# State outputs in four array quarters, the last logits at once, and the surrounding tables

## Chip, cores and metric

The kernel runs on one core of one Trainium2 chip. The metric is the device time of one execution in microseconds; lower is better. The time before is the median of three runs.

## What is computed

The reference is a retention layer (linear attention with a decaying state, written as a loop over time) followed by a mixture of experts in which every token goes to exactly one expert:

```python
# B, H, S, D = 4, 8, 768, 64
for t in range(S):
    state = gamma * state + k[:, :, t] (x) v[:, :, t]
    y[:, :, t] = scale * q[:, :, t] . state
x = y as (B*S, H*D) = (3072, 512)
logits = x @ w_gate                      # 8 experts
order = argsort(-logits.flatten())       # greedy, 384 tokens per expert
for each expert e:
    out[its tokens] = relu(x[its tokens] @ w1[e]) @ w2[e]    # 512 -> 1024 -> 512
```

## The kernel before

**Retention in chunks.** A unit is one batch of the four and one chunk of 128 time steps of the six, so there are 24 units, chunk by chunk (`units`, number 4c + b). Heads go in four pairs: 128 partitions hold the 64 features of two heads. The first eight units are worked one at a time (groups 0 to 7), the other sixteen in pairs (groups 8 to 15). Within a group g, TensorE (PE) does in this order: `scores` of the group that comes next (L297: keys times queries, two row halves of the array side by side), `outputs` of g (L326: queries times the state `T`, which is a 128 x 128 block-diagonal tile for each head pair), `mix` of g (L339: values times masked scores, two column halves, added to the same PSUM tile `yp`), and the state's increment (L353, into `sp`). All are float32, and each such matmul is two instructions in the trace. After every second group the gate of a finished chunk follows (L402, four batches side by side in four column quarters), and one group later its logits are turned (L408).

**The other engines.** VectorE (DVE) multiplies the scores by the decay mask (L300, `am`), adds `sp` to the state (L359, one instruction for each half of the partitions, since only the diagonal blocks of `T` are kept up), and turns some of the finished outputs into rows of `xs` in DRAM (`row_blocks`, L390). GpSimd (POOL) scales queries and keys (L308 `qs`, L304 `ks`). ScalarE (ACT) copies `yp` out of PSUM (L346; in the last chunk half of it goes by DVE, L343 and L344).

**The queue.** All loads and row stores are issued by SyncE (SP), in program order: the loads of the units eight ahead (L268; `ld` has eight buffers) behind a group's work, then four stores for each row block that `ROWS` names for this group (L394). `ROWS = {8: 2, 9: 2, 10: 3, ...}` means two row blocks behind group 8, and so on.

**Logits and search.** `aside` runs between `outputs` and `mix`. It turns the logits of a chunk and prepares the search, and once the first `KNOWN` = 3 chunks are known it finds their largest and smallest logit (`span_parts`: `over_tokens`, `over_partitions`, `grids`), one part at a time, and makes from it the grid of thresholds on which the search counts. If a count never fits, a flag sends the kernel through a slower exact path (`settle`). In the last chunk `gate_last` computes logits unit by unit, straight with tokens on partitions (L367: eight matmuls for two units, 8 columns each), behind the other work of group 15 for units 20 and 21, and after `mix` for 22 and 23. Then the first count is made (L496), and the search for the first expert's threshold runs while PE turns the ten row blocks that are left (`BESIDE`, `rows_out`, L373) and does warming matmuls (`fill`).

**The experts.** From about 124 us on, the eight experts run their two products on PE. The change does not touch this part but for its start, where `HOT` warming matmuls run until the first rows of `xs` are fetched.

Of the kernel before, what the change touches and what calls it, by code (L numbers as in the profile page):

```python
# [7 lines left out]
F32 = mybir.dt.float32  # L8
# [4 lines left out]
AF = mybir.ActivationFunctionType  # L13
# [25 lines left out]
PARTS = 5  # L39
WARM = (10, 4, 4, 4, 0)  # L40
QB = (6, 6, 6)
KNOWN = 3
DEEP = 8
ROWS = {8: 2, 9: 2, 10: 3, 11: 1, 12: 3, 14: 3}
HOT = 22
BESIDE = ((4, 0), (1, 0), (4, 0), (1, 0), (0, 6), (0, 10))
LEFT = sum(k for k, _ in BESIDE)
BETWEEN = 1
BITS = (6, 6, 5, 5, 5, 5)
SHIFT = tuple(32 - sum(BITS[:i + 1]) for i in range(len(BITS)))  # L50
# [3 lines left out]
def tile_retention_moe(ctx: ExitStack, tc: tile.TileContext, qkv, wg, idm, w1, w2,  # L54
# [12 lines left out]
        return cs[:, o:o + w]  # L67

    ident = consts.tile([128, 128], F32, name="ident")
    wgf = consts.tile([128, HP, 32], F32, name="wgf")  # L70
    sw = ctx.enter_context(tc.tile_pool(name="sw", bufs=1))

    onesb = sw.tile([128, 128], BF, name="onesb")
# [164 lines left out]

    yctx = ExitStack()
    yk = yctx.enter_context(tc.tile_pool(name="yk", bufs=1, side="right"))  # L240
    xo = yctx.enter_context(tc.tile_pool(name="xo", bufs=6, side="right"))
    rctx = ExitStack()
    ld = rctx.enter_context(tc.tile_pool(name="ld", bufs=DEEP))
    rc = rctx.enter_context(tc.tile_pool(name="rc", bufs=1))
# [3 lines left out]
    dm = rc.tile([128, 2, HP, C], F32, name="dm")  # L248
    qtb = rc.tile([128, NC, HP, C], F32, name="qtb")
    ktb = rc.tile([128, NC, H], F32, name="ktb")  # L250
    T = [rc.tile([128, HP, 128], F32, name=f"T{b}") for b in range(B)]
    LD, YS = {}, {}
    warm = rc.tile([128, 256], BF, name="warm")
    nc.vector.memset(warm, 0.0)
# [60 lines left out]

    yps = {}

    def outputs(us):

        c = units[us[0]][1]  # L320
        for u in us:
            yp = yps[u] = rp.tile([128, HP, C], F32, name="yp", bufs=2)
            if c:
# [4 lines left out]
            else:  # L328
                busy(WARM[u + 1], yp[:, 0:2, :].rearrange("p a b -> p (a b)"))

    def mix(us):

        c = units[us[0]][1]
        for u in us:
            b, am, yp = units[u][0], st[u][0], yps.pop(u)
            v_ = LD[u][:, 2].rearrange("p (h d) -> p h d", h=H)
            for pr in range(HP):
                for s in range(2):
                    nc.tensor.matmul(yp[64 * s:64 * s + 64, pr, :], v_[:, 2 * pr + s, :], am[:, s, pr, :],  # L339
                                     start=(not c and pr == 0), stop=(pr == HP - 1), skip_group_check=True)  # L340
            YS[b, c] = yk.tile([128, HP, C], F32, name=f"ys{b}_{c}")
            if c == NC - 1:
                nc.scalar.activation(YS[b, c][:, 0:2], yp[:, 0:2], AF.Copy)  # L343
                nc.vector.tensor_copy(YS[b, c][:, 2:4], yp[:, 2:4])  # L344
            else:
                nc.scalar.activation(YS[b, c], yp, AF.Copy)  # L346
        if c < NC - 1:
            sp = rp.tile([128, 2, HP, D], F32, name="sp")
            for i, u in enumerate(us):
                v_ = LD[u][:, 2].rearrange("p (h d) -> p h d", h=H)  # L350
                for pr in range(HP):
                    for s in range(2):
# [8 lines left out]
    lt5 = []  # L361

    def gate_last(b):
        if not b:
            lt5.append(rp.tile([128, 64, E], F32, name="sp"))
        for pr in range(HP):
            nc.tensor.matmul(lt5[0][:, b, :], YS[b, NC - 1][:, pr, :], wgf[:, pr, 0:E], start=(pr == 0),  # L367
                             stop=(pr == HP - 1))
# [10 lines left out]
    def row_out(pr_, i):  # L379
        b, c = units[i]  # L380
        xr = xo.tile([128, DM], F32, name="xr")
        nc.scalar.activation(blocks(xr), pr_.rearrange("p (b a r) -> p b a r", a=4, b=HP), AF.Copy)
        t0 = (b * NC + c) * 128
        nc.sync.dma_start(xs[t0:t0 + 128, :], xr)

    def row_blocks(i):

        b, c = units[i]
        xr = xo.tile([128, DM], F32, name="xr")
        nc.vector.transpose(xr.rearrange("p (t b r) -> p b t r", t=4, b=HP),  # L390
                            YS[b, c].rearrange("p b (t c) -> p b t c", t=4))
        t0 = (b * NC + c) * 128
        for a in range(4):
            nc.sync.dma_start(xs[t0:t0 + 128, 128 * a:128 * a + 128].rearrange("(t c) f -> c t f", t=4),  # L394
                              xr[32 * a:32 * a + 32].rearrange("p (t f) -> p t f", t=4))

    def gate(c):

        gl = rp.tile([128, 512], F32, name="gl")
        for pr in range(HP):  # L400
            for b in range(B):
                nc.tensor.matmul(gl[32 * b:32 * b + 32, 0:C], wgf[:, pr, :], YS[b, c][:, pr, :], start=(pr == 0),  # L402
                                 stop=(pr == HP - 1), skip_group_check=True)
        nc.scalar.activation(gs[c % 2], gl[:, 0:C], AF.Copy)

# [18 lines left out]
    m0, a0, oh0, cmp0 = prep_tiles()  # L424
    parts, whole, ended = None, [], None
    rowed = 0
    nu = len(units)
    groups = [[u] for u in range(2 * B)] + [[u, u + 1] for u in range(2 * B, nu, 2)]

    def aside():  # L430

        nonlocal parts, whole, ended
        if ended is not None:
            c, ended = ended, None
            logit(c)
            if c == 0:
                consts_on_chip()
            cols = slice(c, COLS, NC)
            best(L[:, cols], cols, m0, oh0)()
            codes(cols, oh0, a0)  # L440
            whole.append(cols)
            if c == KNOWN - 1:
                parts = list(span_parts(rc, rp))
        if parts:
            parts.pop(0)()
        elif parts == []:
            for cols in whole:
                reach(cols, B, m0, cmp0, grid[0])
            whole = []

    with tc.manual_schedule(engines={nc.vector.engine, nc.scalar.engine}):
        decays()
        busy(WARM[0], wp[:, 0:256])
        st[0] = scores(0)
        for g, us in enumerate(groups):
            ahead = groups[g + 1] if g + 1 < len(groups) else ()
            if g != B - 1:
                for u in ahead:
# [12 lines left out]
            if g in (B - 1, B):  # L471
                for u in ahead:
                    st[u] = scores(u)
            for u in us:
                if u + DEEP < nu:
                    load(u + DEEP)
            for _ in range(ROWS.get(g, 0)):
                row_blocks(rowed)
# [12 lines left out]
        f()  # L491
        c0 = rp.tile([1 << QB[0], E], F32, name="gl")
        sg0 = sw.tile([1 << QB[0], E], BF, name="sg")
        order = [c for k in range(NC) for c in range(k, COLS, NC)]
        for k, c in enumerate(order):
            nc.tensor.matmul(c0, cmp0[:, c, :], oh0[:, c, :], start=(k == 0), stop=(k == COLS - 1))  # L496
        nc.vector.tensor_copy(L[:, cols], Lc)
        few(c0, sg0)
    rctx.close()
# [664 lines left out]
```

## Time and profile before

| | us |
|---|---|
| median of three runs | 443.43 (442.95 to 445.39) |
| the profiled execution, its own time | 445.22 |
| its span, first to last instruction | 443.4 |
| retention: the last `mix` is issued out at | about 101.4 |
| first search, rows and fetches | about 103 to 124 |
| experts | about 124 to 443 |

The page gives busy time for each engine: PE 427.8 us (96% of the span), DVE 300.8, ACT 142.2, POOL 142.9. PE is nearly always busy, in every stage; whether a PE instruction costs time must therefore be read from what the next one waited for. Times in the views are counted from the span's start. In a timeline row the second number is the length of the merged piece, and the bracket tells how long the engine idled before it and what ended that.

### The profile page before, as it was taken

What the parts mean: (1) busy time and instruction counts of PE and PEld (TensorE: products, weight loads), DVE (VectorE), ACT (ScalarE), POOL (GpSimd) and SP (SyncE); (2) the same over time, 40 slices, a digit from 0 to 9 for tenths busy, and PEclk for the clock granted to TensorE, in tenths of its full rate; (3) what the DMA queues carried; (4) which work ended last, traced back from release to release, by engine and by line L of the source; (5) the groups of instructions that cost most, each with busy time, mean ns of one, the idle gap of its engine ahead of it and who ended that gap; (6) DMA issues with size and microseconds to landing.
All of it is one profiled execution on the core that took longest, in us unless ns stands there. A gap on an engine that the chain in (4) does not pass through costs nothing.

```text
span 443.4 us, 9124 instructions
## 1 busy us (share of the span) xinstructions
PE 427.8 (96%) x3745; PEld 372.2 (84%) x3747; DVE 300.8 (68%) x714; ACT 142.2 (32%) x221; POOL 142.9 (32%) x154
## 2 busy tenths in 40 slices
PE   9998999899989999999899999999999999999994
PEld 7887999898579778977797798789779989989983
DVE  1668689976798759875885888588668926416500
ACT  1111121203245226313431432434244436326301
POOL 2475665110340170034116216134103615402001
PEclk9999999998999999999999999999999999999999
DMA  7999888744673265138126436425703732831001
GB/s 256 410 414 417 328 261 259 215 92 132 237 231 127 97 191 236 27 133 312 54 95 218 186 120 212 169 59 167 296 26 119 229 152 77 302 143 47 1 25 53
DMA packets 23332, 78.99 MB, mean 178 GB/s; under 512 B 3058, under 2 KB 10866, under 8 KB 16884
## 3 DMA queue, kind: packets, MB, share of 16 engines
q0 software_dynamic: 8592, 46.14, 29.8%
q1 hardware_dynamic: 14692, 32.20, 20.7%
q8 instruction: 31, 0.51, 0.5%
q14 instruction: 17, 0.14, 0.1%
HBM read 65.75 MB, written 12.58 MB: 177 GB/s over the span
## 4 chain that ended last, share of the span: by engine, by line
PE 72%; issue 12%; DVE 9%; POOL 2%; DMA 1%; ACT 1%; POOLq 0%; SPq 0%; DVEq 0%
PE ph L869 22%; PE py L890 21%; PE psm L128 6%; PE sc L297 5%; PE yp L339 4%; PE yp L326 3%; PE ph L837 3%; PE sp L353 2%; DVE am L300 2%; POOL out L898 1%; PE gl L314 1%; DVE w2l L128 1%; POOL wraw L785 1%; DMA xg<-xs,idx 1%; PE gl L402 1%
## 5 line engine op out<-in xcount | busy, mean ns | idle before, releaser
L869 PE MATMUL ph<-xh,w1h 128*128 128x384 f32 x256 | 84.3, 343 | 0.5 <-ACT xh L842 0.5
L869 PE MATMUL ph<-xlo,w1h 128*128 128x384 f32 x256 | 82.7, 337 | 1.7 <-DVE xlo L128 1.5
L869 PE MATMUL ph<-xh,w1l 128*128 128x384 f32 x256 | 82.1, 335 | 0.0
L890 PE MATMUL py<-w2h,hh 128*128 128x512 f32 x192 | 78.9, 411 | 0.0
L890 PE MATMUL py<-w2l,hh 128*128 128x512 f32 x192 | 75.4, 393 | 0.6 <-DVE w2l L128 0.6
L890 PE MATMUL py<-w2h,hl 128*128 128x512 f32 x192 | 75.3, 392 | 0.0
L898 POOL DMA_INDIRECT out<-yo,oix x24 | 28.4, 1182 | 125.4 <-ACT yo L896 124.8
L873 ACT ACTIVATE hh<-ph 128x384 fp32r<-128x384 f32 x64 | 31.4, 491 | 77.5 <-PE ph L869 75.8
L785 POOL DMA_INDIRECT wraw<-w,wix x31 | 34.4, 1109 | 51.1 <-DVE un L128 38.1
L869 PEld LDWEIGHTS ph<-xlo,w1h 128*128 128x128 f32 x256 | 47.5, 188 | 2.3 <-DVE xlo L128 2.3
L869 PEld LDWEIGHTS ph<-xh,w1h 128*128 128x128 f32 x256 | 47.8, 188 | 1.6 <-ACT xh L842 0.7
L869 PEld LDWEIGHTS ph<-xh,w1l 128*128 128x128 f32 x256 | 47.7, 188 | 0.0
L128 DVE SCALAR_TENSOR_TENSOR hl<-ph,hh 128x384 fp32r<-128x384 f32 x64 | 34.7, 552 | 16.9 <-ACT hh L873 16.6
L128 DVE TENSOR_TENSOR w1l<-wraw,w1h 128x1024 fp32r<-128x1024 f32 (+1 forms) x36 | 39.2, 1099 | 7.1 <-ACT w1h L803 7.1
L890 PEld LDWEIGHTS py<-w2h,hl 128*128 128x128 f32 x192 | 36.0, 188 | 7.8
L890 PEld LDWEIGHTS py<-w2l,hh 128*128 128x128 f32 x192 | 36.2, 188 | 7.6 <-DVE w2l L128 1.7
L896 ACT ACTIVATE yo<-py 128x512 f32<-128x512 f32 x24 | 14.4, 598 | 86.6 <-PE py L890 47.1
L890 PEld LDWEIGHTS py<-w2h,hh 128*128 128x128 f32 x192 | 36.1, 188 | 6.9 <-issue 0.7
L824 POOL DMA_INDIRECT xg<-xs,idx x24 | 27.6, 1149 | 43.3 <-PE ph L869 28.7
L128 DVE TENSOR_TENSOR w2l<-wraw,w2h 128x1024 fp32r<-128x1024 f32 x32 | 38.7, 1217 | 1.7 <-ACT w2h L803 1.7
L803 ACT ACTIVATE w1h<-wraw 128x1024 fp32r<-128x1024 f32 (+1 forms) x36 | 33.7, 959 | 7.8 <-DMA wraw<-w,wix 7.8
L300 DVE TENSOR_TENSOR am<-sc,dm 128x512 f32<-128x512 f32 x48 | 30.1, 684 | 5.1 <-PE sc L297 4.7
(145 smaller groups left out, 613.2 us busy)
## 6 DMA issues: line engine op xcount, KB each, us to landing
ld<-qkv SPq DMA_DIRECT2D x19, 1024.0 KB, 9.5
xs<-xr SPq DMA_DIRECT2D x56, 64.0 KB, 3.9
ld<-qkv SPq DMA_DIRECT2D x4, 768.0 KB, 5.8
xs<-xr SPq DMA_DIRECT2D x10, 256.0 KB, 2.8
qtb<-qtab SPq DMA_DIRECT2D x5, 256.0 KB, 11.5
ld<-qkv SPq DMA_DIRECT2D x2, 512.0 KB, 5.2
wraw<-w,wix POOLq DMA_INDIRECT x33
xg<-xs,idx POOLq DMA_INDIRECT x24
```

The source lines that it names most:

```text
L128: return f(o, *a, **k)
L297: nc.tensor.matmul(sc[s][:, pr, :], k_[r, w], q_[r, w], start=True, stop=True)
L300: nc.vector.tensor_tensor(am[:, s], sc[s], dm[:, s], op=OP.mult)
L339: nc.tensor.matmul(yp[64 * s:64 * s + 64, pr, :], v_[:, 2 * pr + s, :], am[:, s, pr, :], start=(not c and pr == 0), stop=(pr == HP - 1), s ...
L785: nc.gpsimd.indirect_dma_start(out=t, out_offset=None, in_=w1v if nm == "w1" else w2v, in_offset=bass.IndirectOffsetOnAxis(ap=wix[:, hf:hf ...
L803: nc.scalar.activation(p[0], p[2], AF.Copy)
L824: nc.gpsimd.indirect_dma_start(out=t, out_offset=None, in_=xs, in_offset=bass.IndirectOffsetOnAxis(ap=found[n][0][:, j:j + 1], axis=0))
L869: nc.tensor.matmul(ph, a[:, o:o + 128], x_[:, d], start=(k == 0), stop=(k == 11))
L873: nc.scalar.activation(hh[:, f], ph, AF.Relu)
L890: nc.tensor.matmul(py, h_[:, f, t], a[:, o:o + DM], start=(k == 0), stop=(k == 23))
L896: nc.scalar.activation(yo, py, AF.Copy)
L898: sct = nc.gpsimd.indirect_dma_start(out=out, out_offset=bass.IndirectOffsetOnAxis(ap=oix[:, j:j + 1], axis=0), in_=yo, in_offset=None, bo ...
```

## The change

Six edits, in the words of the diff. `T` keeps only the 64 x 64 block of each head (128 x 64 for a pair) and `outputs` issues for each pair and unit two matmuls of 64 rows by 64 columns. For odd batches the two halves go to swapped halves of `yp` (`half`), so the two units of a group together address the four quarters of the array; the gate has a second copy of its weights with the halves swapped, and the row stores swap them back. The state's update is one DVE instruction. The last chunk's logits come from the same `gate` as the others, after the last `mix`, through a copy and a transpose. The row blocks are dealt out anew (`ROWS`, `TURNED`), one is moved ahead of the first count's end, and `xr` has ten buffers. The logits' range is taken from two chunks, and its parts run in groups that turn no logits.

```diff
-KNOWN = 3
+KNOWN = 2
-ROWS = {8: 2, 9: 2, 10: 3, 11: 1, 12: 3, 14: 3}
-HOT = 22
-BESIDE = ((4, 0), (1, 0), (4, 0), (1, 0), (0, 6), (0, 10))
+ROWS = {8: 4, 9: 1, 10: 3, 11: 2, 13: 2, 14: 2}
+HOT = 25
+BESIDE = ((4, 0), (1, 0), (4, 0), (0, 1), (0, 6), (0, 10))
+TURNED = (1, 3, 5, 0, 7, 2, 4, 9, 11, 6, 13, 15, 17, 19)
...
-    wgf = consts.tile([128, HP, 32], F32, name="wgf")
+    wgf = consts.tile([128, 2, HP, 32], F32, name="wgf")
-    xo = yctx.enter_context(tc.tile_pool(name="xo", bufs=6, side="right"))
+    xo = yctx.enter_context(tc.tile_pool(name="xo", bufs=10, side="right"))
-    T = [rc.tile([128, HP, 128], F32, name=f"T{b}") for b in range(B)]
+    T = [rc.tile([128, HP, D], F32, name=f"T{b}") for b in range(B)]
...
+    def half(s, b):
+
+        o = 64 * (s ^ (b & 1))
+        return slice(o, o + 64)
...
-                for pr in range(HP):
-                    nc.tensor.matmul(yp[:, pr, :], T[b][:, pr, :], qs[:, pr, :], start=(pr == 0), stop=False,
-                                     skip_group_check=True)
...
+        for pr in range(HP if c else 0):
+            for u in us:
                 b, qs = units[u][0], st[u][1]
+                for s in range(2):
+                    r = slice(64 * s, 64 * s + 64)
+                    nc.tensor.matmul(yps[u][half(s, b), pr, :], T[b][r, pr, :], qs[r, pr, :], start=(pr == 0),
+                                     stop=False, skip_group_check=True)
...
-                for s in range(2):
-                    r = slice(64 * s, 64 * s + 64)
-                    nc.vector.tensor_tensor(T[b][r, :, r], T[b][r, :, r], sp[r, i], op=OP.add)
+                nc.vector.tensor_tensor(T[b], T[b], sp[:, i], op=OP.add)
...
-                if g == len(groups) - 1:
-                    for u in groups[g - 1]:
-                        gate_last(units[u][0])
-                aside()
+                aside(g)
...
-        for u in groups[-1]:
-            gate_last(units[u][0])
         c = NC - 1
-        cols, Lc = slice(c, COLS, NC), lt5[0][:, 0:B]
+        gate(c)
+        c0 = rp.tile([1 << QB[0], E], F32, name="sc0", bufs=2)
+        order = [c for k in range(NC) for c in range(k, COLS, NC)]
+
+        def first(k0, k1):
+            for k in range(k0, k1):
+                nc.tensor.matmul(c0, cmp0[:, order[k], :], oh0[:, order[k], :], start=(k == 0), stop=(k == COLS - 1))
+
+        first(0, 8)
+        lt = rp.tile([128, 512], F32, name="sp")
+        nc.tensor.transpose(lt[:, 0:128], gs[c % 2], ident)
+        cols, Lc = slice(c, COLS, NC), lt[:, 0:128].rearrange("p (b x) -> p b x", b=B)[:, :, 0:E]
+        first(8, COLS - B)
         f = best(Lc, cols, m0, oh0)
+        pr_ = rp.tile([128, DM], F32, name="sc1", bufs=2)
+        row_part(pr_, rest[0], 0, HP)
+        row_out(pr_, rest.pop(0))
         reach(cols, B, m0, cmp0, grid[0])
         f()
```

PE in group 9, between the scores of the next group and `mix` (`yp` is the output tile, `qs` the scaled queries, `T_109` and `T_110` the states of batches 2 and 3). Before:

```order
L326 MATMUL yp<-qs,T_109 128x128 x4
L326 MATMUL yp<-qs,T_110 128x128 x4
L408 MATMUL gl<-ident,gs_143 128x128
L339 MATMUL yp<-am,ld 64x128 x16
L353 MATMUL sp<-ld,ks 64x64 x16
```

and now:

```order
L335 MATMUL yp<-qs,T_109 64x128 x2
L335 MATMUL yp<-qs,T_110 64x128 x2
L335 MATMUL yp<-qs,T_109 64x128 x2
L335 MATMUL yp<-qs,T_110 64x128 x2
L335 MATMUL yp<-qs,T_109 64x128 x2
L335 MATMUL yp<-qs,T_110 64x128 x2
L335 MATMUL yp<-qs,T_109 64x128 x2
L335 MATMUL yp<-qs,T_110 64x128 x2
L410 MATMUL gl<-ident,gs_143 128x128
L346 MATMUL yp<-am,ld 64x128 x16
L360 MATMUL sp<-ld,ks 64x64 x16
```

Eight matmuls of 128 columns out became sixteen of 64, and the two units take turns pair by pair.

SP from the loads of units 16 and 17 on (`ld` is a unit's load, `xs` a row store). Before:

```order
L268 DMA ld<-qkv 128x2048 x2
L394 DMA xs<-xr 32x4x128 x8
L268 DMA ld<-qkv 128x2048 x2
L276 DMA qtb<-qtab 128x512
L394 DMA xs<-xr 32x4x128 x8
L268 DMA ld<-qkv 128x1536 x2
L394 DMA xs<-xr 32x4x128 x12
L268 DMA ld<-qkv 128x1536 x2
L394 DMA xs<-xr 32x4x128 x28
L384 DMA xs<-xr 128x512 x10
```

and now:

```order
L268 DMA ld<-qkv 128x2048 x2
L396 DMA xs<-xr 32x4x128 x16
L268 DMA ld<-qkv 128x2048 x2
L276 DMA qtb<-qtab 128x512
L396 DMA xs<-xr 32x4x128 x4
L268 DMA ld<-qkv 128x1536 x2
L396 DMA xs<-xr 32x4x128 x12
L268 DMA ld<-qkv 128x1536 x2
L396 DMA xs<-xr 32x4x128 x24
L385 DMA xs<-xr 128x512 x10
```

Eight stores more stand ahead of the second pair of loads, four more ahead of the third and of the fourth.

PE in group 15, the last (`ys_5_...` are the outputs of chunk 5). Before:

```order
L326 MATMUL yp<-qs,T_109 128x128 x4
L326 MATMUL yp<-qs,T_110 128x128 x4
L367 MATMUL sp<-wgf,ys_5_1354 128x8 x4
L367 MATMUL sp<-wgf,ys_5_1365 128x8 x4
L408 MATMUL gl<-ident,gs_142 128x128
L339 MATMUL yp<-am,ld 64x128 x16
L367 MATMUL sp<-wgf,ys_5_1440 128x8 x4
L367 MATMUL sp<-wgf,ys_5_1451 128x8 x4
```

and now:

```order
L335 MATMUL yp<-qs,T_110 64x128 x2
L410 MATMUL gl<-ident,gs_142 128x128
L346 MATMUL yp<-am,ld 64x128 x16
L404 MATMUL gl<-ys_5_1412,wgf 32x128
L404 MATMUL gl<-ys_5_1423,wgf 32x128
L404 MATMUL gl<-ys_5_1491,wgf 32x128
L404 MATMUL gl<-ys_5_1502,wgf 32x128
```

The four `L404` rows stand four times; no gate matmul is left ahead of `mix`, and the fourth row of the first round reads the unit that `mix` ends with.

## Rows read from the trace of the kernel before

**Rows 1.** Busy time by stretch, groups 10 and 13 (PE, PEld, DVE, ACT, POOL, clock, DMA).
```profile
57.51:65.32 7.81, 7.81 (x148) 7.30 (x145) 6.33 (x13) 1.20 (x2) 5.56 (x6) 1.00 0.75 254
80.14:88.70 8.56, 7.28 (x120) 6.84 (x116) 8.21 (x25) 1.47 (x3) 1.34 (x2) 1.00 0.82 247
```

**Rows 2.** Timeline of PE, group 10 and the start of group 11.
```profile
57.51 2.06 PE L297 MATMUL sc<-ld 64*128 64x128 f32 x32
59.50 2.05 PE L326 MATMUL yp<-qs,T 128*128 128x128 f32 x16
61.48 1.97 PE L339 MATMUL yp<-am,ld 128*64 128x128 f32 x32
63.28 1.10 PE L353 MATMUL sp<-ld,ks 128*64 128x64 f32 x32
64.31 1.08 PE L402 MATMUL gl<-ys,wgf 128*32 128x128 f32 x32
65.32 2.06 PE L297 MATMUL sc<-ld 64*128 64x128 f32 x32
```

**Rows 3.** Timeline of PE, group 6: the state's increment waits for DVE.
```profile
37.63 0.69 PE L353 MATMUL sp<-ld,ks 128*64 128x64 f32 x16 [1.93 <-DVE T L359]
```

**Rows 4.** Groups of instructions by line, 42.5 to 104 us: DVE's updates and row blocks.
```profile
L359 DVE TENSOR_TENSOR T<-T,sp 64x256 f32<-64x256 f32 x26 | 10.9, 418 | 7.1 <-PE sp L353 6.9
L390 DVE STREAM_TRANSPOSE xr<-ys 128x512 f32<-128x512 f32 x14 | 9.0, 687 | 0.2
```

**Rows 5.** Timeline of all engines, group 13: PE's broadcast of the range.
```profile
85.56 0.38 PE L218 MATMUL gl<-ident,topb 2*128 2x2 f32 x2 [1.28 <-DVE L L409]
```

**Rows 6.** Timeline of SP's issues, 47 to 107 us.
```profile
49.28 0.80 SPq L268 DMA_DIRECT2D ld<-qkv  x2
52.20 6.83 SPq L394 DMA_DIRECT2D xs<-xr  x8
59.15 0.87 SPq L268 DMA_DIRECT2D ld<-qkv  x2
...
69.95 0.93 SPq L268 DMA_DIRECT2D ld<-qkv  x2
...
79.92 0.88 SPq L268 DMA_DIRECT2D ld<-qkv  x2
```

**Rows 7.** SP's waits over the span: us in total, times, longest.
```profile
SPq L394 <- DMA ld<-qkv: 12.3, 6, 3.3
```

**Rows 8.** Timeline of POOL: queries of units 21, 22 and 23, ended by their loads.
```profile
77.19 1.30 POOL L308 TENSOR_TENSOR qs<-ld,qtb 128x512 f32<-128x512 f32 x1 [0.40 <-DMA ld<-qkv]
85.41 1.28 POOL L308 TENSOR_TENSOR qs<-ld,qtb 128x512 f32<-128x512 f32 x1 [6.92 <-DMA ld<-qkv]
88.64 1.35 POOL L308 TENSOR_TENSOR qs<-ld,qtb 128x512 f32<-128x512 f32 x1 [1.96 <-DMA ld<-qkv]
```

**Rows 9.** Timeline of all engines, group 15 and the first logits after it.
```profile
95.77 0.28 ACT L404 ACTIVATE gs<-gl 128x128 f32<-128x128 f32 x1 [0.71 <-PE gl L402]
...
97.46 1.85 PE L367 MATMUL sp<-wgf,ys 128*128 128x8 f32 x16
99.17 0.31 PE L408 MATMUL gl<-ident,gs 128*128 128x128 f32 x1
...
101.84 0.42 DVE L344 COPY ys<-yp 128x256 f32<-128x256 f32 x1 [0.45 <-ACT ys L343]
103.29 0.19 DVE L128 TENSOR_REDUCE m<-sp 128x4 f32<-128x32 f32 x1 [1.03 <-PE sp L367]
```

**Rows 10.** The chain, 103 to 117 us: a row block's four transposes on PE.
```profile
106.00 0.85 PE py L373 x4
...
110.00 0.59 PE py L373 x4
```

**Rows 11.** Busy time by stretch, columns as in rows 1: clock behind the last gate.
```profile
101.40:104.80 3.40, 2.85 (x41) 2.83 (x41) 1.55 (x7) 0.38 (x1) 0.00 (x0) 1.00 0.31 63
104.80:108.20 3.40, 3.40 (x17) 3.28 (x16) 2.70 (x7) 1.66 (x3) 0.00 (x0) 0.50 0.21 76
```

More of the change, by code (lines that the diff above doesn't have):

```diff
@@ L41 @@
 QB = (6, 6, 6)
-KNOWN = 3
+KNOWN = 2
 DEEP = 8
-ROWS = {8: 2, 9: 2, 10: 3, 11: 1, 12: 3, 14: 3}
-HOT = 22
-BESIDE = ((4, 0), (1, 0), (4, 0), (1, 0), (0, 6), (0, 10))
-LEFT = sum(k for k, _ in BESIDE)
+ROWS = {8: 4, 9: 1, 10: 3, 11: 2, 13: 2, 14: 2}
+HOT = 25
+BESIDE = ((4, 0), (1, 0), (4, 0), (0, 1), (0, 6), (0, 10))
+TURNED = (1, 3, 5, 0, 7, 2, 4, 9, 11, 6, 13, 15, 17, 19)
 BETWEEN = 1
@@ L321, in outputs @@
         for u in us:
-            yp = yps[u] = rp.tile([128, HP, C], F32, name="yp", bufs=2)
-            if c:
-                b, qs = units[u][0], st[u][1]
-                for pr in range(HP):
-                    nc.tensor.matmul(yp[:, pr, :], T[b][:, pr, :], qs[:, pr, :], start=(pr == 0), stop=False,
-                                     skip_group_check=True)
-            else:
-                busy(WARM[u + 1], yp[:, 0:2, :].rearrange("p a b -> p (a b)"))
+            yps[u] = rp.tile([128, HP, C], F32, name="yp", bufs=2)
+            if not c:
+                busy(WARM[u + 1], yps[u][:, 0:2, :].rearrange("p a b -> p (a b)"))
+        for pr in range(HP if c else 0):
+            for u in us:
+                b, qs = units[u][0], st[u][1]
+                for s in range(2):
+                    r = slice(64 * s, 64 * s + 64)
+                    nc.tensor.matmul(yps[u][half(s, b), pr, :], T[b][r, pr, :], qs[r, pr, :], start=(pr == 0),
+                                     stop=False, skip_group_check=True)
     def mix(us):
@@ L338, in mix @@
                 for s in range(2):
-                    nc.tensor.matmul(yp[64 * s:64 * s + 64, pr, :], v_[:, 2 * pr + s, :], am[:, s, pr, :],
+                    nc.tensor.matmul(yp[half(s, b), pr, :], v_[:, 2 * pr + s, :], am[:, s, pr, :],
                                      start=(not c and pr == 0), stop=(pr == HP - 1), skip_group_check=True)
@@ L356, in mix @@
                 b = units[u][0]
-                for s in range(2):
-                    r = slice(64 * s, 64 * s + 64)
-                    nc.vector.tensor_tensor(T[b][r, :, r], T[b][r, :, r], sp[r, i], op=OP.add)
[L361 to L368, printed above, removed]
+                nc.vector.tensor_tensor(T[b], T[b], sp[:, i], op=OP.add)
     def row_part(pr_, i, d0, d1):
@@ L381, in row_out @@
         xr = xo.tile([128, DM], F32, name="xr")
-        nc.scalar.activation(blocks(xr), pr_.rearrange("p (b a r) -> p b a r", a=4, b=HP), AF.Copy)
+        to, of = blocks(xr), pr_.rearrange("p (b a r) -> p b a r", a=4, b=HP)
+        if b & 1:
+            for z in range(2):
+                nc.scalar.activation(to[:, :, 2 * z:2 * z + 2], of[:, :, 2 - 2 * z:4 - 2 * z], AF.Copy)
+        else:
+            nc.scalar.activation(to, of, AF.Copy)
         t0 = (b * NC + c) * 128
@@ L393, in row_blocks @@
         for a in range(4):
-            nc.sync.dma_start(xs[t0:t0 + 128, 128 * a:128 * a + 128].rearrange("(t c) f -> c t f", t=4),
+            f0 = 128 * (a ^ 2 * (b & 1))
+            nc.sync.dma_start(xs[t0:t0 + 128, f0:f0 + 128].rearrange("(t c) f -> c t f", t=4),
                               xr[32 * a:32 * a + 32].rearrange("p (t f) -> p t f", t=4))
@@ L401, in gate @@
             for b in range(B):
-                nc.tensor.matmul(gl[32 * b:32 * b + 32, 0:C], wgf[:, pr, :], YS[b, c][:, pr, :], start=(pr == 0),
+                nc.tensor.matmul(gl[32 * b:32 * b + 32, 0:C], wgf[:, b & 1, pr, :], YS[b, c][:, pr, :], start=(pr == 0),
                                  stop=(pr == HP - 1), skip_group_check=True)
@@ L426, in tile_retention_moe, with aside @@
     rowed = 0
+    rest = [u for u in range(len(units)) if u not in TURNED]
+    rest.sort(key=lambda u: (u & 1, u))
     nu = len(units)
     groups = [[u] for u in range(2 * B)] + [[u, u + 1] for u in range(2 * B, nu, 2)]
-    def aside():
+    def aside(g):
         nonlocal parts, whole, ended
[L433 to L436, printed above, removed]
+        new = ended
+        if new is not None:
+            logit(new)
+            if new == 0:
                 consts_on_chip()
-            cols = slice(c, COLS, NC)
+            cols = slice(new, COLS, NC)
             best(L[:, cols], cols, m0, oh0)()
@@ L441, in aside @@
             whole.append(cols)
-            if c == KNOWN - 1:
+            ended = None
+            if new == KNOWN - 1:
                 parts = list(span_parts(rc, rp))
-        if parts:
+                parts.pop(0)()
+        elif parts:
             parts.pop(0)()
-        elif parts == []:
+            return
+        if parts == [] and (new is None or g == len(groups) - 1):
             for cols in whole:
@@ L477, in tile_retention_moe @@
             for _ in range(ROWS.get(g, 0)):
-                row_blocks(rowed)
+                row_blocks(TURNED[rowed])
                 rowed += 1
@@ L484, in tile_retention_moe @@
                     ended = c1
-        for u in groups[-1]:
-            gate_last(units[u][0])
         c = NC - 1
-        cols, Lc = slice(c, COLS, NC), lt5[0][:, 0:B]
+        gate(c)
[9 more added lines that the diff above has]
+        first(8, COLS - B)
         f = best(Lc, cols, m0, oh0)
+        pr_ = rp.tile([128, DM], F32, name="sc1", bufs=2)
+        row_part(pr_, rest[0], 0, HP)
+        row_out(pr_, rest.pop(0))
         reach(cols, B, m0, cmp0, grid[0])
         f()
-        c0 = rp.tile([1 << QB[0], E], F32, name="gl")
         sg0 = sw.tile([1 << QB[0], E], BF, name="sg")
-        order = [c for k in range(NC) for c in range(k, COLS, NC)]
-        for k, c in enumerate(order):
-            nc.tensor.matmul(c0, cmp0[:, c, :], oh0[:, c, :], start=(k == 0), stop=(k == COLS - 1))
+        first(COLS - B, COLS)
         nc.vector.tensor_copy(L[:, cols], Lc)
@@ L904, in mm2, with rows_out @@
             yield 690
-    def rows_out(i):
-        pr_ = pp.tile([128, DM], F32, name="py" if i % 2 else "ph", bufs=2 if i % 2 else PARTS)
+    def rows_out(i, k):
+        pr_ = pp.tile([128, DM], F32, name="py" if k % 2 else "ph", bufs=2 if k % 2 else PARTS)
         row_part(pr_, i, 0, HP)
@@ L942, in tile_retention_moe @@
         for _ in range(rows):
-            rows_out(rowed)
+            rows_out(rest.pop(0), rowed)
             rowed += 1
@@ L1148 @@
     decay, upper, qtab, ktab, thr, cst = _tables()
-    wg = _np.zeros((128, HP, 32), _np.float32)
-    wg[:, :, 0:E] = moe_w_gate.reshape(HP, 128, E).transpose(1, 0, 2)
+    wg = _np.zeros((128, 2, HP, 32), _np.float32)
+    wg[:, 0, :, 0:E] = moe_w_gate.reshape(HP, 128, E).transpose(1, 0, 2)
+    wg[:, 1] = _np.roll(wg[:, 0], 64, axis=0)
     qkv = _np.ascontiguousarray(_np.stack([cols(k), cols(q), rows(v), rows(k)], axis=2))
```

## The prediction

> **What bounds the kernel now.** I read the busy time by stretch first, then PE's timeline of one pair of groups, then who waits for whom. In the retention's paired groups PE has no gap: group 10 lasts 7.81 us and PE is busy for all of it, with DVE at 6.33 and POOL at 5.56 [rows 1]. The timeline shows the parts, start to start: scores 1.99, outputs 1.98, `mix` 1.80, increment 1.03, gate 1.01 [rows 2]. So what is taken off PE there comes off the time, as long as the other engines and the loads keep up. Group 13 is the only one with a hole: 7.28 busy of 8.56 [rows 1], because the broadcast of the range waited 1.28 us for DVE [rows 5].
>
> The loads are the thing to watch. They share SP's queue with the row stores [rows 6], stores wait for earlier loads to land (six times, 12.3 us) [rows 7], and the query scaling of units 22 and 23 starts only when their loads land, 5.5 and 8.7 us after the issue of their pair [rows 6, 8]. Unit 23's landing, 88.6, is just when PE would want it. DMA share is 0.75 to 0.82 [rows 1]: the queue's order more than bandwidth sets these times.
>
> **The parts of the change.**
>
> *Outputs in quarters.* Two units now issue 32 instructions of 128 columns where 16 stood. The rows give prices by how many stand abreast. One at a time: 16 in 1.98, 0.12 each. Two abreast (scores in row halves, `mix` in column halves): 32 in 1.99 and 1.80. Four abreast (the gate, in column quarters): 32 in 1.01 [rows 2]. The four matmuls of a head pair address four different quarters, so I take four abreast, at 1.05, between half of `mix` (0.90) and a little above the gate, since their weights are twice as wide as the gate's. That saves 0.93 in each of eight groups: 7.4 us. Groups 4 to 7 have one unit, whose two quarters go two abreast: as long as now.
>
> *The state's update.* One DVE instruction of 256 elements in place of two (0.418 each [rows 4]): 26 become 13, 5.4 us less on DVE. On the path this counts once, in group 6, where the increment waits for DVE [rows 3]: 0.4 us. The smaller POOL memsets at the start cost nothing. The second copy of the gate's weights is 64 KB more in the loads of the first 40 us, about 0.1 to 0.2; I count it against rounding.
>
> *Last logits.* The matmuls ahead of the last `mix` go: from 97.46 to the next instruction at 99.17 [rows 9], 1.7 us off PE. Behind `mix` the chain gets longer. Now: `mix` issued out at 101.37, the copies end at 102.26, unit 23's logits follow and the first maximum starts at 103.29, 1.9 us behind `mix` [rows 9]. Then: copies (0.9), a whole gate (1.0 [rows 2]), a copy and a transpose (0.28 and 0.31 [rows 9]) with two handovers: about 2.8. That gives 0.9 back.
>
> *Range from two chunks.* Its parts come one chunk earlier and in groups without logits, so the broadcast no longer waits behind them: the 1.28 us [rows 5] go. The grid is still made on DVE, which gains time. The cover would be gone if the range missed a threshold: then the whole slow path runs.
>
> *Rows dealt anew, ten buffers.* DVE turns four blocks behind group 8 rather than two, 2 x 0.69 us more there [rows 4], and gains 0.84 from the update; with the 1.5 us that it has free in a group [rows 1] it keeps up, but only just. Ten buffers remove nothing that shows as a wait. One block more ahead of the first count's last four matmuls: four transposes, 0.59 [rows 10], half hidden by DVE's comparisons: 0.3 lost. One block less ahead of the third count's sum: 0.2 won. Three more warming matmuls fit into the wait for the fetched rows: nothing.
>
> *Clock.* Behind the last gate matmuls PE's granted clock is 0.50 from 104.80 to 108.20, the lower level of 1.2 GHz, after 3.4 us in which it did only matmuls of 8 columns with gaps [rows 11]. There a block takes 0.85 in place of 0.59 [rows 10], and four blocks stand ahead of the second count: 1.0. The new tail has a dense gate and a row block in that place, so I expect full clock and take 0.9; nothing is the other end.
>
> *The queue.* This takes part of the gain back. Pair of loads one (units 16, 17) is issued behind group 8's work: 49.28 less 0.4 and 0.93, 48.0. Eight stores then need until 59, because the last waits for the second load to land [rows 6, 7]; now until 57.7. Then eight more, at 0.5 to 0.85 each (8 took 6.83 with that wait [rows 6]): I take 0.5, so pair two is issued at 61.7, where it was 59.15. By the same 8 to 9 us it lands at 70.4. PE alone would want it for the second scores of group 12 at 72.2 - 0.4 - 4 x 0.93 + 1.0 = 69.1: 1.3 us of waiting. Pair three comes four stores later, at 65 to 67, right behind pair two in the DMA engines, and lands at 75.5. The twelve stores wait for it, four remain, and pair four is issued at about 77.8, only 2.1 earlier than 79.92. Second loads landed 7.2 and 8.7 us after the issue of their pair [rows 6, 8], so unit 23 is there between 85.0 and 86.5; I take 86.0, nearer to its own row, against 88.6. Its scores (1.0) end at 87.0, where they ended at 90.7: 3.7 won so far. Groups 14 and 15 then save 2 x 0.93 and 1.7. The last `mix` comes 7.2 us earlier. PE alone would give 7.4 + 0.4 + 1.7 + 1.3 = 10.8; the loads keep 3.6 of it.
>
> **Sum.** 7.2 won until the last `mix`; then 0.9 and 0.3 lost, 0.9 and 0.2 won: 7.1. The experts behind keep their order. The profiled execution took 445.22, which gives 438.1; the median of the three runs is 1.8 below it, so the time to compare is 443.43 - 7.1 = **436.3 us**.
>
> **Rivals.**
>
> *Loads in time.* If the stores run nearer to 0.45, or the second loads land in 6 us, PE alone sets the retention: 10.8 won, less the tail's 0.1, 432.7. For it: the first load of a pair lands after 5.5 us [rows 6, 8]. Against it: pair four lay on the edge already, and now four more stores stand ahead of it.
>
> *The halves of one unit take turns.* The two row halves of one unit write the same PSUM tile. No row shows this: the scores' row halves write two tiles, `mix`'s column halves use all rows. If they exclude each other, the pair's 32 go two abreast, 1.98 as before, and single units take 1.98 in place of 1.0, of which groups 6 and 7 are on the path (+2.0). Then: 0.4 + 1.7 + 1.3 - 2.0 - 0.1 = 1.3 won, 442.1. The change would not do what it says. The Trainium skill's page "TensorEngine Tiling (Array Packing)", section "Restrictions and Gotchas", speaks for this rival: "Different row tiles cannot access same PSUM bank simultaneously". By that rule the time is 442.1, by the rows of the gate 436.3; no row here decides, because no row has this case.
>
> *Quarters one at a time* (slower). If PE runs each quarter by itself, at the 0.11 of one instruction, a pair takes 3.8, 1.8 more than now, in eight groups: 14.4, and single units 2.0 more in all. Less the 3.3 of the other edits: 13.1 lost, 456.5. It decides from 2.4 us per pair on, where 8 x 0.42 eats the 3.3. Against it: two abreast is seen both by rows and by columns [rows 2].
>
> **Chances and range.** Forecast 0.55, loads in time 0.28, turns 0.11, one at a time (with the slow path) 0.06. Forecast's own bounds: unit 23 as late as now (88.6) leaves 4.5 until the last `mix`, and without the clock 3.6 in all, 439.8; on the other side it meets the first rival, where a pair at 0.95 gives 432. So 432.0 to 440.5 leaves out the last two cases. A measurement of this kernel tells about 0.5%, 2.2 us, from no change: faster means below 441.2. The first two cases are faster, turns is nearly all the same: 0.83, 0.11, 0.06.
>
> **What would show it.** Outputs of a pair at 1.0 to 1.1 from their start to `mix` (2.0 would be the second rival, 3.8 the third). Groups of 6.0 and 6.9 us without a gap, but for PE's waits at the scores of units 19 and 23, with `qs` of unit 23 starting near 86. SP's pairs near 48, 61.7, 66 and 78. No wait at the range's broadcast. First maximum 2.8 us behind the last `mix`, the clock at 1.00 behind it. I am wrong if the outputs take more than 1.4, if the loads' waits are under 1 us in all or over 6, or if a stage behind 124 us changes its length.

## The result, and the profile after

| us | before | after |
|---|---|---|
| median of 20 runs each, side by side | 444.48 (441.71 to 449.15) | 440.88 (437.41 to 443.75) |
| ratio, 95% interval | | 0.9932 (0.9907 to 0.9957) |
| span of the profiled execution | 443.4 | 440.3 |
| group 8's outputs start | 44.79 | 42.34 |
| the last `mix` is issued out | 101.30 | 98.91 |
| first product of the first expert | 127.45 | 124.18 |

The change makes the kernel faster by some 3 us where 7.1 were forecast: the sign is right, and the time lies 0.4 us outside the range. (The ratio leaves out two executions of the kernel before that fell in the chip's slower state, 448.67 and 449.15.) The table already says where to look. At group 8 PE is 2.45 us ahead, and at the end of the retention, eight groups with cheaper outputs later, it is 2.39 us ahead. All that the paired groups should have given was spent inside them. (Of the 2.45, some 1.4 are not the change's but belong to the one execution of before that was profiled; see below, at the state's update.)

PE's timeline of the changed kernel, groups 11, 12 and 14 and the end (start, length, engine, line, the bracket as in the rows of before):

```profile
63.78 1.10 PE L335 MATMUL yp<-qs,T 64*64 64x128 f32 x32
64.82 0.33 PE L410 MATMUL gl<-ident,gs 128*128 128x128 f32 x1
...
69.15 1.16 PE L297 MATMUL sc<-ld 64*128 64x128 f32 x16 [1.18 <-DMA ld<-qkv]
72.08 2.08 PE L297 MATMUL sc<-ld 64*128 64x128 f32 x16 [1.76 <-DMA ld<-qkv]
74.09 1.61 PE L335 MATMUL yp<-qs,T 64*64 64x128 f32 x32
75.63 0.38 PE L218 MATMUL gl<-ident,topb 2*128 2x2 f32 x2
...
89.19 2.08 PE L297 MATMUL sc<-ld 64*128 64x128 f32 x16 [2.14 <-DMA ld<-qkv]
91.20 1.59 PE L335 MATMUL yp<-qs,T 64*64 64x128 f32 x32
92.72 1.97 PE L346 MATMUL yp<-am,ld 128*64 128x128 f32 x32
...
97.01 1.97 PE L346 MATMUL yp<-am,ld 128*64 128x128 f32 x32
98.91 1.64 PE L404 MATMUL gl<-ys,wgf 128*32 128x128 f32 x32
```

Three things are to be read here. A pair's outputs take 1.04 us from start to start (63.78 to 64.82), where [rows 2] had 1.98. PE waits for loads three times, 5.1 us in all, where before it had none. And behind the second and the third of these waits the same work is slower: 16 scores take 2.0 in place of 1.1, outputs 1.5 in place of 1.04. The busy time by stretch (columns as in [rows 1]) shows why:

```profile
68.40:71.80 3.40, 1.16 (x16) 1.00 (x16) 2.88 (x6) 0.00 (x0) 2.26 (x2) 1.00 0.99 354
71.80:75.20 3.40, 3.12 (x36) 2.92 (x40) 1.04 (x2) 0.00 (x0) 2.31 (x3) 0.50 1.05 424
75.20:78.60 3.40, 3.40 (x83) 3.21 (x78) 2.73 (x7) 1.20 (x2) 2.55 (x2) 1.00 0.75 226
85.40:88.80 3.40, 1.65 (x36) 1.39 (x32) 2.80 (x6) 0.28 (x1) 1.29 (x1) 1.00 0.80 268
88.80:92.30 3.50, 3.11 (x38) 2.92 (x42) 1.38 (x3) 0.00 (x0) 1.27 (x1) 0.51 0.41 84
```

Both times the stretch in which PE waited is followed by one with the granted clock at 0.50 or 0.51, the lower level of 1.2 GHz. These two waits were paid twice.

SP's timeline, the counterpart of [rows 6], shows where the loads were:

```profile
45.88 1.02 SPq L268 DMA_DIRECT2D ld<-qkv  x2
47.72 15.52 SPq L396 DMA_DIRECT2D xs<-xr  x16
63.35 0.88 SPq L268 DMA_DIRECT2D ld<-qkv  x2
...
64.80 2.08 SPq L396 DMA_DIRECT2D xs<-xr  x4
66.98 2.48 SPq L268 DMA_DIRECT2D ld<-qkv  x2
72.02 8.26 SPq L396 DMA_DIRECT2D xs<-xr  x12
80.39 0.86 SPq L268 DMA_DIRECT2D ld<-qkv  x2
81.35 19.08 SPq L396 DMA_DIRECT2D xs<-xr  x24
```

The first pair is issued 3.4 us earlier than before and the second 4.2 later; the last comes 0.5 later than in [rows 6]. What SP waited for, against the one row of [rows 7]:

```profile
SPq L396 <- DMA ld<-qkv: 14.3, 7, 3.2
SPq L268 <- DMA ld<-qkv: 9.3, 5, 2.4
```

Of the first, 6.5 us lie between 45 and 66 us; in the kernel before one wait stood there (48 to 61 us). The two answers, after and before:

```profile
SPq L396 <- DMA ld<-qkv: 6.5, 3, 2.2
```

```profile
SPq L394 <- DMA ld<-qkv: 3.2, 1, 3.2
```

In the program every DMA issue of SP and of ACT waits on one of eight completion counters, which are taken in turn, so a store or a load waits until the transfer issued eight places earlier has landed. The trace agrees: the three waits of 6.5 us end with the stores at 51.69, 54.80 and 57.29, each right behind the landing of the load issued eight places earlier (at 40.51, 45.88 and 46.35). Unit 23's queries start when its load is there (POOL, as in [rows 8]), 0.57 later than before:

```profile
89.21 1.27 POOL L308 TENSOR_TENSOR qs<-ld,qtb 128x512 f32<-128x512 f32 x1 [2.25 <-DMA ld<-qkv]
```

### The profile page after: what moved, and what is told of

It reads as the page before. It is cut to its first block, busy times and chain, and to the rows that moved or that the text cites. A ratio compares the mean times of both kernels' runs of the same rounds, so it can differ in the third digit from the quotient of the medians.

```text
span 440.3 us, 9437 instructions
## 1 busy us (share of the span) xinstructions
PE 421.5 (96%) x3912; PEld 362.9 (82%) x3912; DVE 291.3 (66%) x694; ACT 142.5 (32%) x224; POOL 142.1 (32%) x154
## 4 chain that ended last, share of the span: by engine, by line
PE 65%; issue 13%; DVE 8%; DMA 6%; POOL 3%; SPq 2%; ACT 1%; POOLq 0%; DVEq 0%; ACTq 0%
PE ph L883 23%; PE py L904 22%; PE psm L128 6%; DMA ld<-qkv 6%; PE sc L297 4%; PE yp L346 3%; PE ph L851 2%; PE yp L335 2%; SPq L396 2%; POOL out L912 1%; PE sp L360 1%; DVE w2l L128 1%; POOL wraw L799 1%; DMA xg<-xs,idx 1%; DVE am L300 1%
```

## Experiments

My theory: the stores ahead of the last pairs in SP's queue keep the loads late, and the clock falls behind the waits. Rivals: the quarters are worth less than they look; the DMA engines' bandwidth sets the landings. Experiments one to four ran on one chip (before there: 445.18), five to eight on another (442.70), nine on a third (444.32); ratios are to the kernel before on the same chip, times in traces are compared by position.

**One: fewer stores ahead of the loads.** The row blocks are turned later; one block (four stores) stands between two pairs in place of 16, 4 and 12.

```diff
-ROWS = {8: 4, 9: 1, 10: 3, 11: 2, 13: 2, 14: 2}
+ROWS = {8: 1, 9: 1, 10: 1, 11: 4, 12: 3, 13: 2, 14: 2}
```

> The changed kernel with its fourteen row blocks dealt out later: one behind each of groups 8, 9 and 10, then 4, 3, 2 and 2 behind groups 11 to 14, so that 12 stores stand ahead of the last pair of loads on SP in place of 32. Theory (the stores ahead of the loads keep the gain, and the waits for them lower PE's clock): the last pair is issued before 72 us in place of 80.4, PE waits for no load in groups 12 and 14, the clock stays at 1.00 there, the last mix ends near 91 us in place of 98.9, and the kernel is 6 to 8 us faster than the changed one, about 10 us faster than the one before. Rival one (DMA bandwidth, not the order of the queue, makes the loads late): the last pair is issued earlier but lands within 1.5 us of 89, and the time changes by under 1.5 us. Rival two (DVE is the bound once the loads are in time): loads on time, but PE waits for DVE's am in groups 11 to 13, and under 4 us are won.

Measured: 436.27 us, ratio 0.9813 (0.9761 to 0.9864), span 435.0, an interval wholly below the change's. SP's timeline:

```profile
45.65 0.83 SPq L268 DMA_DIRECT2D ld<-qkv  x2
...
53.26 0.83 SPq L268 DMA_DIRECT2D ld<-qkv  x2
...
59.96 2.35 SPq L268 DMA_DIRECT2D ld<-qkv  x2
...
68.62 0.83 SPq L268 DMA_DIRECT2D ld<-qkv  x2
```

The last pair goes out 11.8 us earlier, no PE wait for a load is left in the paired groups, and the last `mix` starts at 90.10 instead of 97.01. Of these 6.9 us the first expert gets 5.7 (118.50): now the clock falls behind the last gate, 0.50 from 96.70 to 100.10. So the late loads were what held the change back: the same loads and stores, in another order, cost 1.2% less.

**Two: outputs unit by unit.** The two quarters of one unit stand abreast, not four of two units.

```diff
-        for pr in range(HP if c else 0):
-            for u in us:
+        for u, pr in [(u, pr) for u in us for pr in range(HP if c else 0)]:
+            if True:
```

> The changed kernel with the quarters issued unit by unit (all of one unit, then all of the other), so that two quarters stand abreast in place of four; the number of instructions is the same. Both theories: the outputs of a pair last about 2.0 us in place of 1.04. Theory (the loads bound the retention): only the two pairs behind the last landing, groups 14 and 15, show it, and PE idles less ahead of the scores of units 19 and 23; 1.5 to 2.5 us slower than the changed kernel. Rival (PE bounds it, and the waits in the trace are slack): eight groups show it, 7 to 8 us slower.

Measured: 440.69, ratio 0.9914 (0.9880 to 0.9948): no difference from the change, against what I expected. PE's timeline:

```profile
65.13 1.59 PE L335 MATMUL yp<-qs,T 64*64 64x128 f32 x32
66.65 0.33 PE L410 MATMUL gl<-ident,gs 128*128 128x128 f32 x1
...
74.47 1.88 PE L297 MATMUL sc<-ld 64*128 64x128 f32 x16 [3.57 <-DMA ld<-qkv]
...
89.40 2.06 PE L297 MATMUL sc<-ld 64*128 64x128 f32 x32
```

A pair takes 1.52 here (2.0 was expected), 0.48 more than four abreast. The eight pairs cost 3.8 us more and none of it shows at the end: the wait for unit 19 is longer, but PE reaches unit 23 later, its load is there, and the wait of 2.14 and the fall of the clock behind it are gone. While loads set the pace, PE's saving is waiting time.

**Three: the waits filled.** Warming matmuls ahead of the scores of units 18, 19 and 23.

```diff
+        if u in WARMED:
+            busy(WARMED[u], sc[0][:, 0:2, :].rearrange("p a b -> p (a b)"))
...
+WARMED = {18: 8, 19: 14, 23: 18}
```

> The changed kernel with warming matmuls of 256 columns ahead of the scores of units 18, 19 and 23 (8, 14 and 18 of them, at most 0.9, 1.5 and 2.0 us at full clock), so that PE does not stand idle there. Theory (the wait for unit 23 also lowers the clock, which costs 1.0 us in its scores and 0.5 in the outputs behind): the clock stays at 1.00 from 86 to 93 us, and 1.0 to 1.8 us are won; the first fall, near 72 us, goes too but wins nothing, since the later wait takes it up. Rival (the clock falls whatever PE does while it waits, or it costs nothing): no difference beyond 0.5 us, or the kernel slower by the matmuls.

Measured: 439.16, ratio 0.9884 (0.9842 to 0.9926). The stretch that stood at 0.51 above:

```profile
88.80:92.30 3.50, 3.50 (x69) 2.97 (x69) 2.40 (x5) 0.00 (x0) 1.24 (x1) 1.00 0.55 110
```

Unit 23's scores start at 89.27, as late as in the change (89.19), so the load is no earlier; but they take 1.09 instead of 2.01, and the last `mix` starts at 95.69, 1.3 earlier. At group 12 nothing stayed: its broadcast comes at 75.86 (75.63 in the change), since this execution had reached group 10's gate 2.1 us later. The time's interval overlaps the change's; it is the trace that shows the clock's price in this execution.

**Four: the old deal** of row blocks in the changed kernel.

```diff
-ROWS = {8: 4, 9: 1, 10: 3, 11: 2, 13: 2, 14: 2}
+ROWS = {8: 2, 9: 2, 10: 3, 11: 1, 12: 3, 14: 3}
```

> The changed kernel with the row blocks dealt out by the old table (2, 2, 3, 1, 3, 3 behind groups 8, 9, 10, 11, 12 and 14), all else as in the change: 28 stores ahead of the last pair of loads in place of 32, 8 ahead of the second in place of 16. Theory (the order of the queue): pair two is issued near 58 us in place of 63.4, the last pair near 77 in place of 80.4, and 2 to 4 us are won against the changed kernel. Rival (each pair of loads needs its 8 to 10 us whatever stands between): the last pair within 1 us of 80.4, and under 1 us of difference.

Measured: 439.92, ratio 0.9894 (0.9854 to 0.9934); again an overlap. The pairs go out at 45.92, 56.56, 67.59 and 79.23: the second is 6.8 us earlier than in the change, 0.85 for each of the eight stores that are gone there; the last is only 1.2 earlier (the theory said 77, the rival within 1 us of 80.4), and PE waits all the same:

```profile
84.32 1.16 PE L297 MATMUL sc<-ld 64*128 64x128 f32 x16 [2.40 <-DMA ld<-qkv]
87.64 2.08 PE L297 MATMUL sc<-ld 64*128 64x128 f32 x16 [2.16 <-DMA ld<-qkv]
```

The clock falls here too (0.50 from 88.40 to 91.80). So not the new deal alone was too early; the old one, with 8, 8 and 12 stores between the pairs, is too early as well, once PE is faster.

**Five: the late deal in the kernel before** (the edit of experiment one).

> The kernel before, with the row blocks dealt late as in the first experiment. Theory (before, PE sets the retention's time and the loads only just keep up; the late deal is worth something only where outputs in quarters have made PE faster): 0 to 1 us faster than before, ratio 0.997 to 1.001; SP's pairs of loads near 46, 54, 62 and 70, the scores of unit 23 still 90 us or later. Rival (the late deal is good by itself, whatever PE does): 3 to 5 us faster, ratio 0.989 to 0.993.

Measured: 442.23, ratio 0.9995 (0.9968 to 1.0023): nothing. The last pair goes out at 70.52, 9.4 us earlier, and the last `mix` starts 0.6 earlier. Even that is not the deal's: group 8's outputs had started 1.38 earlier (43.41), ahead of all that the deal moves, and from there to the last `mix` this execution takes 0.8 longer, 0.55 of it a wait for DVE's copy in group 15. The theory holds, but for its detail on unit 23, whose scores came at 88.5 instead of 90. There PE set the time; the deal matters only beside the quarters.

**Six: late deal and outputs unit by unit** (the edits of one and two together).

> The first experiment's late deal, and the outputs issued unit by unit (two quarters abreast) as in the second. Theory (four abreast is worth 8 x 0.48 us, and this showed nothing in the second experiment only because the loads ate it): 3 to 4 us slower than the late deal alone, ratio to before 0.988 to 0.991; outputs of a pair 1.5 us, no wait of PE for a load in the paired groups. Rival (something else than the loads paces the groups, so how many stand abreast does not matter): ratio to before 0.981 to 0.983 as with the late deal alone.

Measured: 434.55, ratio 0.9820 (0.9783 to 0.9856), the rival's number. But the theory's rows are there too: outputs of 1.52, no wait for a load. The last `mix` starts at 91.21, 1.1 us later than with the late deal alone. Of the 3.8 us that four abreast saves there, 2.6 went into other small gaps: 1.3 at the increment of group 10, where the profile names no releaser, 0.6 at the scores ahead of that group's outputs, and 0.7 in group 15, at DVE's copy.

```profile
61.62 0.27 PE L360 MATMUL sp<-ld,ks 128*64 128x64 f32 x1 [1.28 <-issue]
...
88.48 1.42 PE L335 MATMUL yp<-qs,T 64*64 64x128 f32 x32 [0.27 <-DVE ys L351]
```

(Rows of experiment one.) The rest was lost behind the gate, where the clock of experiment one fell and that of six did not. So both expectations missed: the loads are in time, and still four abreast gives little over two.

**Seven: late deal, and seven warming matmuls behind the last gate.**

```diff
         first(8, COLS - B)
+        wt = rp.tile([128, 512], F32, name="gl")
+        busy(3, wt[:, 0:256])
...
         first(COLS - B, COLS)
+        busy(4, wt[:, 0:256])
```

> The late deal, and seven warming matmuls in PE's idle time behind the last gate, three ahead of the last row block and four behind the first count. Theory (with the late deal the granted clock is 0.50 from 96.7 to 100.1 because PE is little used in the 3.4 us ahead of it; at 1.00 four row blocks take 0.6 in place of 1.05 and the count 0.6 less): clock 1.00 throughout, 0.5 to 1.5 us faster than the late deal, ratio to before 0.977 to 0.980. Rival (the search behind it waits for DVE, so PE's clock there costs nothing, or the matmuls delay the count): within 0.5 us of the late deal.

Measured: 433.91, ratio 0.9807 (0.9771 to 0.9842), span 430.8. The same stretch of experiment one and, in the second fence, of this kernel:

```profile
96.70:100.10 3.40, 3.40 (x27) 3.07 (x26) 2.36 (x6) 2.39 (x4) 0.00 (x0) 0.50 0.76 207
```

```profile
96.70:100.10 3.40, 3.21 (x44) 2.76 (x43) 2.65 (x9) 2.37 (x5) 0.00 (x0) 1.00 0.89 285
```

From the last `mix` to the first expert 26.97 in place of 28.40. The trace shows the 1.4 us; the ratio, beside 0.9813, can't tell them. It has the lowest median of all kernels run, below both that were compared, but from six and seven I would not say which is faster.

**Eight: the row stores issued by ACT**, the loads by SP.

```diff
-            nc.sync.dma_start(xs[t0:t0 + 128, f0:f0 + 128].rearrange("(t c) f -> c t f", t=4),
+            nc.scalar.dma_start(xs[t0:t0 + 128, f0:f0 + 128].rearrange("(t c) f -> c t f", t=4),
```

> The changed kernel with its own deal, but the stores of the row blocks that DVE turned are issued by ACT, so that SP's queue holds only loads until the retention ends. Theory (the order of SP's queue makes the last pairs late, not the bandwidth): pairs of loads issued as soon as their buffers are free, near 46, 53, 60 and 68; no wait of PE for a load in groups 12 and 14; the last mix 4 to 6 us earlier, unless ACT's copies of the outputs come late behind stores that wait, which would show as PE waiting for ACT; ratio to before 0.980 to 0.985 in the good case. Rival (bandwidth: loads and stores share the 16 DMA engines, and the loads take as long in any queue): the second load of a pair lands 10 us or more behind its issue, PE waits 2 us as in the changed kernel, ratio 0.990 to 0.995.

Measured: 459.85, ratio 1.0399 (1.0358 to 1.0439), far outside both. ACT's copy of the logits stood behind stores that waited, three times for 30.7 us in all, and PE behind it:

```profile
61.97 0.47 PE L410 MATMUL gl<-ident,gs 128*128 128x128 f32 x1 [11.11 <-ACT gs L406]
```

The experiment says nothing on bandwidth; it shows what a queue costs that an engine with work on the path has to serve.

**Nine: the loads issued by ACT**, the stores by SP.

```diff
-            nc.sync.dma_start(LD[u][:, w0:w1_], qkv[u, :, w0:w1_])
+            (nc.scalar if u >= 16 else nc.sync).dma_start(LD[u][:, w0:w1_], qkv[u, :, w0:w1_])
...
-            nc.sync.dma_start(qtb[:, c + 1], qtab[:, c + 1])
+            (nc.scalar if u >= 16 else nc.sync).dma_start(qtb[:, c + 1], qtab[:, c + 1])
```

> The changed kernel with its own deal of row blocks; the loads of units 16 to 23 (and the query table's next part) are issued by ACT in place of SP, so that no store stands ahead of them, while the stores stay on SP. Theory (in the changed kernel it is the stores ahead of them in SP's queue that hold the last pairs back, not the DMA engines' bandwidth): pairs issued when their buffers are free, near 46, 53, 60 and 67; second loads 7 to 9 us behind; no wait of PE for a load in groups 12 and 14; last mix 4 to 6 us earlier than in the changed kernel, ratio to before 0.979 to 0.985. Rival (bandwidth: 16 stores and a pair of loads need the DMA engines for longer than two groups last, in whatever queues): pairs issued early but the second load lands 10 us or more behind its issue, PE waits for units 19 and 23 as in the changed kernel, ratio 0.990 to 0.995.

Measured: 441.83, ratio 0.9940 (0.9910 to 0.9971). The time is the rival's, the reason is neither's. ACT's timeline and waits:

```profile
57.54 1.30 ACTq L268 DMA_DIRECT2D ld<-qkv  x2
...
63.46 1.08 ACT L353 ACTIVATE ys<-yp 128x512 f32<-128x512 f32 x2 [10.04 <-DMA xs<-xr]
```

```profile
ACT ys L353 <- DMA xs<-xr: 19.2, 2, 10.0
```

No store stands ahead of a load in ACT's queue, and its issues still wait for stores to land, since the eight counters are shared. PE no longer waits for the loads of units 19 and 23, but 3.28 us for ACT, and the clock falls to 0.50 behind that. So this experiment does not settle the question of bandwidth. The DMA share of the changed kernel says more:

```profile
45.00:50.00 5.00, 4.88 (x116) 4.30 (x114) 3.68 (x8) 0.99 (x3) 3.31 (x3) 1.00 1.02 412
50.00:55.00 5.00, 4.55 (x103) 4.00 (x94) 4.86 (x11) 1.20 (x2) 4.06 (x4) 1.00 0.97 379
55.00:60.00 5.00, 5.00 (x105) 4.58 (x105) 4.27 (x11) 0.62 (x2) 2.59 (x3) 1.00 0.49 119
60.00:65.00 5.00, 5.00 (x127) 4.39 (x123) 4.10 (x8) 0.85 (x2) 2.57 (x3) 1.00 0.55 98
```

To 55 us the engines are full, and the first pair's loads of 1 MB land 2.5 us apart: there bandwidth sets the landings. From 55 to 65, while the second pair stands behind the stores, they are half idle; and when the second and third pair go out 3.6 us apart, they are full again (0.99 and 1.05 from 68.4 to 75.2, above). In experiment one they are full from 45 to 65 (1.00 to 1.04) and the loads are in time. The order decides whether the half-idle time is used. That is read from the shares; no run here lightens the full stretches alone.

## Why the prediction was right and wrong

- *Outputs in quarters*: right. 1.05 was taken, 1.04 came; both rivals on the array (1.98 and 3.8) fall. The rule that the prediction quoted from the Trainium skill, "TensorEngine Tiling (Array Packing)", section "Restrictions and Gotchas", would have given 1.98; here two row tiles that write one PSUM tile did not take turns. Experiment two is the plainest case: the two halves of one unit follow each other alone, and a pair took 1.52, where one at a time (0.12 each) it would be 3.8.
- *The state's update*: right in size, with luck on top. 0.4 was forecast; the wait in group 6 [rows 3] fell from 1.93 to 0.16, and group 8 came 2.45 earlier. But in experiment five, on another chip, where the kernel is that of before up to there, the same wait is 0.40 and group 8 starts at 43.41, 1.38 earlier than in the profile of before. Ahead of the update DVE works off a row of small instructions of 0.15 to 0.2 us. Some of them ended only with a POOL instruction beside them: four in the profile of before (1.02, 1.27, 0.72 and 1.19 us), two in experiment five (1.04 and 1.27) and two in the changed kernel (0.99 and 1.21). Two of the four in before, then one of the same instructions and PE's wait in experiment five:

```profile
32.76 1.27 DVE L98 CAST tokc<-cs 128x24 bf16<-128x24 f32 x1
35.31 1.19 DVE L128 TENSOR_TENSOR eqc<-oh,codeo 128x32 bf16<-128x32 bf16 x1
```

```profile
34.95 0.17 DVE L128 TENSOR_TENSOR eqc<-oh,codeo 128x32 bf16<-128x32 bf16 x1
36.24 0.69 PE L353 MATMUL sp<-ld,ks 128*64 128x64 f32 x16 [0.40 <-DVE T L359]
```

  So about 1.1 of the 2.45 belong to the change (part of it the cheaper outputs of single units), and 1.4 are luck of the execution that was compared.
- *Range and last logits*: right. L218 starts at 75.63 without a wait, and nothing but the logits' transpose stands between outputs and the last `mix`.
- *The tail*: 0.9 won where 0.1 was to be lost. The first maximum came 2.44 behind `mix` (forecast 2.8, before 1.99), and the row blocks behind it ran at full clock as said: four blocks ahead of the second count in 1.9 us against 3.5, so 1.6 where 0.9 was taken.
- *The queue* is the step that failed: "Then eight more, at 0.5 to 0.85 each (...): I take 0.5", and what hangs on it, the issue of pair four and the landing of unit 23. The first eight stores ended at 57.6, as forecast (57.7), although pair one went out 2.1 earlier than forecast: all three waits for landings, 6.5 us, lie among them. The second eight had no such wait and took 5.66 up to pair two, 0.71 each. One of them stood 2.20 in its issue with no wait recorded; the median of the issues is 0.43. SP's timeline, cut between the eights and at that store:

```profile
47.72 9.87 SPq L396 DMA_DIRECT2D xs<-xr  x8
57.69 5.55 SPq L396 DMA_DIRECT2D xs<-xr  x8
```

```profile
60.57 2.20 SPq L396 DMA_DIRECT2D xs<-xr  x1
```

  So pair two came at 63.35 (forecast 61.7). Pair three's second load waited for pair two's first to land, and landed at 77.2 (forecast 75.5). The stores from there to pair four took 3.2 (forecast 2.3), 1.1 of it a wait that the profile puts down to DVE (L223): pair four at 80.39 (forecast 77.8). Unit 23 landed 8.8 later (forecast 8.2), at 89.2, not 86.0.
- *A term that was missing*: the clock behind the waits. Scores 2.01 for the 1.0 of the sum and outputs 1.52 for 1.04 make 1.5 us behind unit 23. This is the profiled execution, with a mean granted clock of 0.988 and a time of 442.12; over the 20 executions the mean clock goes from 0.985 to 0.999, and the two with the highest (0.996 and 0.999) took 437.41 and 439.38. So the falls are not the same in every execution.

So the last `mix` was to be issued out at 94.2 and was at 98.9: 3.2 by the landing, 1.5 by the clock. The tail gave 0.9 back. Experiment one tests the first of these by itself, three the second. The waits stayed in the 1 to 6 us that I allowed, but I priced them by their length alone. The rival "loads in time" gave 432.7, a ratio of 0.976; with the late deal the loads are in time and the ratios are 0.981 to 0.982. So its 10.8 us for PE alone was too much as well: from group 8's outputs to the last `mix` issued out it is 49.9 us in experiment one and 56.5 before, 6.6 less where 10.4 (outputs, last logits, range) were counted. The small gaps listed under experiment six are part of the rest.

What stays open: why one store's issue took 2.20 us, why some small DVE instructions ended only with POOL's, and the 1.28 us without a releaser in experiment one (the same instruction waits 0.73 in seven and not at all in six).

## What to carry to other kernels

Where an engine is made faster, first move the loads' issues ahead by as much: here the same edit of the deal is worth nothing in the kernel before (0.9995) and about 1.2% in the changed one. Where a price read from rows is a range (0.5 to 0.85 for a store), work the sum with both ends, and price a wait of TensorE by its length and by the slower work behind it. Moving issues to ACT's queue did not help here: ACT has copies on the path, and its issues wait on the same completions. Before a gain is booked from two traces, look in a third whether the same stage varies without it: here it did, by 1.4 us.

## What the runs showed of the hardware

- Two quarters abreast took 1.52 us for 32 matmuls (experiment two), less than the 1.80 and 1.99 of the pairs in [rows 2]; four took 1.04 (the changed kernel).
- Some small DVE instructions took 0.7 to 1.3 us in place of 0.2 beside a POOL instruction and ended with it (four in the profile of before, between 31.75 and 36.50 us); the wait behind them was 1.93 us there and 0.40 in experiment five, where two did.
- The granted clock fell to 0.50 right behind PE's waits for loads of 1.8 and 2.1 us (from 71.80 and 88.80) and stood at 1.00 again in the next stretch; with 40 warming matmuls in the waits it was at 1.00 from 71.8 to 95.7 throughout (experiment three).
